# Gating the weight transfers of a DeltaNet and Fourier-mixing kernel on TensorE's instruction packets, in a hand-written list scheduler

## The chip, the cores and the metric

The kernel runs on one core of one Trainium2 chip. The metric is the device time of one launch in microseconds; lower is better. TensorE (PE) does the matrix products, VectorE (DVE), ScalarE (ACT) and GpSimd (POOL) the elementwise work, and SyncE (SP) issues nearly all transfers from and to HBM. Each engine runs its own instruction list in the order in which it was written.

## The reference

Two blocks follow each other. The first is a delta-rule attention over 4 batches, 8 heads, 768 positions and a head size of 48; the second mixes its output (4 x 768 x 384) with a two-dimensional Fourier transform, normalizes it and runs a two-layer MLP.

```python
k_n = k / (np.linalg.norm(k, axis=-1, keepdims=True) + 1e-06)
for t in range(S):
    y[:, :, t] = np.einsum('bhd,bhde->bhe', q[:, :, t], state)
    v_old = np.einsum('bhde,bhd->bhe', state, kt)
    state = state + bt[:, :, :, None] * np.einsum('bhd,bhe->bhde', kt, vt - v_old)
...
mixed = np.real(np.fft.fft(np.fft.fft(x, axis=1), axis=2))
u = x + mixed
un = (u - mu) / np.sqrt(var + 1e-06)
ch = np.maximum(un @ w_ch1, 0.0) @ w_ch2
return (u + ch).astype(np.float32)
```

The weights `w_ch1` (384 x 1536) and `w_ch2` (1536 x 384) come as 64-bit floats, which the chip turns into 32-bit ones by integer arithmetic; everything else is float32.

## The kernel before

The sequence of each batch is cut into six units of 128 positions, each of two chunks of 64; there are 24 units. A unit loads its k, q and v (192 KB each, `load`), transposes them on TensorE (`turn`, line 467), builds small triangular systems for the heads (`keys`, `gram`), inverts them on DVE (`invert16`, `invert`) and then runs the recurrence chunk by chunk (`chain0`, `values0`, `outputs0` for the first six units, `step` and `outputs` for the others). When a batch's units are done, `mixing` runs its Fourier transform (`folds`, `seq`, `feat`), normalizes (`normed`) and runs the MLP in three groups of 256 rows (`mlp`; the last batch's `mlpw`). An MLP group takes six blocks of the first layer (12 matmuls of 128x256 in the trace each) and six of the second; the blocks of the first layer are evicted by a Relu at line 1459.

Nothing of this is written in the order in which it runs. Each function hands its pieces to a planner, `Plan.op`, with the engines that could run it, an estimated duration, the memory that it reads and writes, a due time, the size of a transfer (`kb`) or the number of TensorE instructions (`ni`). `Plan.schedule` then simulates all engines at build time, picking for each free engine the most urgent piece that is ready, and `issue` writes the instructions out in that order. All matmuls go through the helper lines 464 and 467, all copies through 473 and 475. The order is fixed when the kernel is built; on the chip the semaphores decide when each instruction goes.

Parts of the planner that the change touches:

- `Plan.fetch` models TensorE's instruction packets: 256 instructions each. A packet is asked for when TensorE has gone AHEAD = 128 instructions past a boundary and is there FETCH = 3.4 us later; TensorE cannot pass the next boundary before.
- `Plan.speed` and `Plan.work` model TensorE's clock by stretches of 3.413 us; `Plan.light` tells when TensorE has had little work in the last 2.6 us.
- `idle` (lines 1899 to 1914) writes filler matmuls on constants into a spare PSUM bank: groups of six at the very start (line 1906, 12 matmul rows in the trace), a pair on 64 rows or a single one on 128 rows later (line 1913). They compute nothing that is used. The planner adds one where TensorE has nothing ready and its load is light.
- TARGET, FORCE, GAP, GAP2, HALF, PLOOK, PEND, HOLD and the due-time constants M0 to MD are numbers that steer these choices.

The weights are brought in by `weights`, 18 pieces of 512 columns, nine for each matrix, in the order w1, w2, w1, w2, w1, w2 by thirds. A piece is transferred as 64-bit words into a staging slot (512 KB, on SP, line 512; in two transfers where it crosses a row block), and converted by six operations: ACT (1675), DVE (1678), ACT (1681), DVE (1686), POOL (1691) and DVE (1694). The staging slots are parts of tiles that are not in use yet: seven for the first NW = 14 pieces (`ws`, two in `x`, four in the tiles R1 and R0), and then three (`ws` and two in `x`). A transfer is written in SP's order at the place where the planner found its slot free; in the program it waits for the last reader of the slot.

```python
stages = [(ws, 0), (xs[1], 0), (xs[1], 1024), (R1, 2304), (R1, 3328), (R0, 0), (R0, 1024)]

def where(nw):
    return stages[nw[0] % 7] if nw[0] < NW else stages[(nw[0] - NW) % 3]
```

Of the kernel before, what the change touches and what calls it, by code (L numbers as in the profile page):

```python
# [14 lines left out]
ACT = mybir.ActivationFunctionType  # L15
# [9 lines left out]
class Op:  # L25
    __slots__ = ("i", "engs", "fn", "deps", "succ", "pr", "mode", "banks", "new", "lat",
                 "ndep", "ready", "start", "end", "eng", "due", "kb", "col", "ni", "hot", "port")
# [3 lines left out]
RATE = 190.0  # L31
WIN, WARM, COLD, BUSY, CLOCK = 3.413, 610.0, 619.0, 200.0, True
LOOK, HOLD, EARLY = 1e9, 0.2, 25.7
FOLD, BY, SEQ, HOT, HOTPE, HOTPK, HOTG, NORM = 1, 1, 2, 1.0, 1, 1, 0, 1
HOTC, PORT, E2 = 2, 1, 5.0
GAP, HALF = 0.15, 90.0
GAP2 = 0.324
PLOOK, PHOLD, PEND = 22.2, 0.367, 110.0
NHALF = 1
FORCE = 546.3  # L40
BLOCK, AHEAD, FETCH = 256, 128, 3.4
TARGET, SPANW = 725.1, 2.6


class Plan:
# [10 lines left out]
    def op(self, engs, fn, rd=(), wr=(), pr=0.0, mode=None, new=None, use=(), lat=0.0,  # L56
           due=1e9, kb=0, col=0, ni=0, port=False):
# [5 lines left out]
        o.due, o.kb, o.col, o.ni, o.hot, o.port = due, kb, col, ni, self.hot, port  # L63
        o.banks = list(use) + new
# [55 lines left out]
    def fetch(self, o):  # L120

        n0, n1 = self.count, self.count + o.ni
        for k in range((n0 - AHEAD) // BLOCK + 1, (n1 - AHEAD) // BLOCK + 1):

            t = o.start + (o.end - o.start) * (k * BLOCK + AHEAD - n0) / o.ni
            self.come.append(max(t, self.come[-1]) + (FETCH if t > 12 else 7.0))
        for k in range(n0 // BLOCK + 1, n1 // BLOCK + 1):
            if k < len(self.come):
                o.end = max(o.end, self.come[k] + (o.end - o.start) * (n1 - k * BLOCK) / o.ni)
        self.count = n1  # L130
# [19 lines left out]
    def schedule(self, pick, limits, switch, idle=None, span=()):  # L150
# [26 lines left out]
        self.count, self.come = 64, [0.0, 0.0]  # L177
        done, n, now = 0, len(ops), 0.0
        order, strict, last = [], True, None
        while done < n:  # L180
            progressed = False
            for e in self.ENG:
# [4 lines left out]
                if e != "PE":  # L187
                    cand = [o for o in cand if not any(b.busy > now + 1e-9 and (not BY or b.by != e)
                                                       for b in o.banks)]
                if e == "PE":  # L190
# [42 lines left out]
                elif cand:  # L233
                    if PORT and e == "DVE" and free["POOL"] > now + 1e-9:
                        cand = [o for o in cand if not o.port]
# [19 lines left out]
                dur = o.engs[e]  # L255
                if e == "PE":
                    dur *= self.speed(now)
                    if mode is not None:
                        dur += switch.get((mode, o.mode), 0.0)
                    mode = o.mode  # L260
                    for b, s in zip(o.new, fr[len(o.new), o.mode] if o.new else ()):
                        b.slot, slots[s] = s, None
                        self.half = {k: x for k, x in self.half.items() if x != s}
                        held[b.cls] = held.get(b.cls, 0) + 1
                o.start, o.end, o.eng = now, now + dur, e
                if o.kb:

                    o.end = max(now, landed[-8]) + dur
                    moved = max(moved, o.end) + o.kb / RATE
                    landed.append(moved + o.lat)  # L270
                    o.lat = landed[-1] - o.end
# [94 lines left out]
def kernel(  # L366
# [90 lines left out]
    def eng(e):  # L457
        return {"DVE": nc.vector, "POOL": nc.gpsimd, "ACT": nc.scalar, "SP": nc.sync}[e]

    def I(x):  # L460
        kp(x)
# [54 lines left out]
    M0, MP, MX, MN, MA, MT, MD = 100.7, 138.9, 27.6, 31, 25, 7.59, 5.46  # L516
# [1128 lines left out]
    def weights(src, dst, rows, cols, where, pr, pieces=None):  # L1645
# [10 lines left out]
        for c0 in pieces:  # L1656
# [6 lines left out]
            rr = st[:, 0:2 * n:2]  # L1663
            done = 0
# [44 lines left out]
    NW, IV, IV1, WP = 14, 9.46, 10, -25.4  # L1709
# [152 lines left out]
    mixing(0)  # L1862
    for ro in ros[2:]:
        if ro is ros[-1]:
            tables(0)
        prepare(ro)
        consume(ro)

    LIM = {"state": 1, "sum": 4, "attn": 6, "mix": 4, "mlp": 4, "norm": 2, "win": 4}
    WAIT, GATHER, URGENT, FIRST = 5.62, 1.92, 12.1, 10.3  # L1870
    E0, E1, D1 = 1.0, 10.0, 115.0
# [79 lines left out]
```

## Time and profile before

| what | us |
|---|---|
| runs, median of 3 | 677.76 (676.92 to 678.70) |
| profiled execution | 683.04 |
| its span, first to last instruction | 681.2 |
| mean granted TensorE clock over the span | 0.980 |
| first MLP matmul of the first batch (line 464, w and R) | 132.03 |
| last conversion step of a weight (line 1694) | 142.8 |

The profile describes one profiled execution. Its times count from the span's first instruction. "Granted clock" is the share of full speed that TensorE's clock was given in a stretch. A view by stretches cuts the span at given times and tells how long each engine was busy in each. In the view of waits, "<- issue" means that the engine stood still and that the profile shows no semaphore that it waited for. PE's rows count matmuls, PEld its weight loads; in this trace a float32 matmul of the program stands as two matmul and two load rows. SPq is the queue in which SP issues transfers. Queues 8 and 14 of the DMA engines carry instructions, queue 1 the kernel's data. The trace also has the start of each single DMA packet by queue.

### The profile page before, as it was taken

The numbers are of one execution on the slowest core, as the hardware profiler recorded it, in microseconds if no ns is written. First come the engines' busy times: TensorE is split into PE (matmuls) and PEld (weight loads), VectorE is DVE, ScalarE is ACT, GpSimd is POOL, SyncE is SP. The second block draws the span as 40 slices with busy tenths as digits, with TensorE's granted clock in tenths as the row PEclk, the third lists the DMA queues.
The fourth block names the chain that finished last, engine by engine and source line by source line (L and its number), as shares of the span: only waits on it lengthen the run. The fifth ranks groups of instructions, "written<-read, shape, count | busy, mean of one in ns | idle before, by whom it ended". The sixth has DMA issues, their size and how long they took to land.

```text
span 681.2 us, 22852 instructions
## 1 busy us (share of the span) xinstructions
PE 665.9 (98%) x10028; PEld 535.5 (79%) x10028; DVE 471.8 (69%) x1365; ACT 265.3 (39%) x739; POOL 34.0 (5%) x34
## 2 busy tenths in 40 slices
PE   7999979999999999999999999999999999999998
PEld 7778879867777777877777869776877778899997
DVE  3999467999996268999962546999995433823133
ACT  5679575622344324522433514322523412311110
POOL 3013321100000000000000000000000000000000
PEclk9999696999999999999999999999999999999999
DMA  9925465000032212000312210000000000000000
GB/s 215 276 76 132 87 162 137 2 1 1 25 62 51 58 26 50 24 1 2 72 38 48 61 37 13 24 2 1 27 1 4 26 1 1 24 1 24 0 25 23
DMA packets 82581, 31.33 MB, mean 46 GB/s; under 512 B 75569, under 2 KB 79634, under 8 KB 82354
## 3 DMA queue, kind: packets, MB, share of 16 engines
q1 hardware_dynamic: 82290, 29.65, 17.6%
q8 instruction: 78, 1.28, 0.8%
q10 hardware_dynamic: 192, 0.23, 0.1%
q14 instruction: 21, 0.17, 0.1%
HBM read 25.16 MB, written 4.72 MB: 44 GB/s over the span
## 4 chain that ended last, share of the span: by engine, by line
PE 92%; DVE 4%; issue 2%; ACT 2%; DVEq 0%; ACTq 0%
PE pp L464 87%; PE pp L467 3%; PE pp L1913 1%; DVE tmp L839 1%; DVE w L845 1%; PE pp L1906 1%; ACT us L473 1%; DVE rr L862 0%; DVE rr L735 0%; DVE rr L779 0%; DVE w L805 0%; DVE us L698 0%; ACT L1723 0%; ACT w L473 0%; DVE w L812 0%
## 5 line engine op out<-in xcount | busy, mean ns | idle before, releaser
L464 PE MATMUL pp<-R,w 128*128 128x256 f32 x864 | 203.5, 387 | 0.6 <-ACT R L473 0.6
L464 PEld LDWEIGHTS pp<-R,w 128*128 128x128 f32 x864 | 161.2, 191 | 24.1 <-ACT R L473 0.7
L464 PE MATMUL pp<-w,R 128*128 128x384 f32 x432 | 151.8, 495 | 0.0
L464 PEld LDWEIGHTS pp<-w,R 128*128 128x128 f32 x432 | 79.0, 190 | 46.0 <-issue 0.2
L1459 ACT ACTIVATE R<-pp 128x512 f32<-128x512 f32 x54 | 32.2, 597 | 132.4 <-PE pp L464 128.5
L473 ACT ACTIVATE us<-pp 128x256 f32<-128x256 f32 (+3 forms) x165 | 58.2, 393 | 42.9 <-PE pp L464 24.7
L464 PE MATMUL pp<-us 64*64 64x48 f32 (+3 forms) x2496 | 63.1, 238 | 2.8 <-issue 2.8
L464 PEld LDWEIGHTS pp<-us 64*64 64x64 f32 (+1 forms) x2496 | 53.6, 137 | 9.5 <-issue 7.0
L922 DVE TENSOR_TENSOR rr<-rr,tmp 128x210 f32<-128x210 f32 (+11 forms) x180 | 58.3, 327 | 3.4
L917 DVE TENSOR_TENSOR tmp<-rr 128x210 f32<-128x210 f32 (+12 forms) x180 | 58.1, 326 | 3.0
L464 PEld LDWEIGHTS pp<-u,us 64*64 64x64 f32 x1472 | 41.9, 138 | 19.0 <-issue 16.9
L464 PE MATMUL pp<-u,us 64*64 64x48 f32 x1472 | 48.2, 225 | 3.8 <-issue 3.3
L1174 DVE TENSOR_TENSOR u<-u,pp 64x192 f32<-64x192 f32 x66 | 22.5, 350 | 34.6 <-PE pp L464 31.6
L1238 DVE TENSOR_TENSOR x<-x,pp 64x192 f32<-64x192 f32 x66 | 23.2, 352 | 29.2 <-PE pp L464 28.1
L473 ACT ACTIVATE x<-pp 64x192 f32<-64x192 f32 (+1 forms) x81 | 25.0, 324 | 44.4 <-PE pp L464 39.7
L1572 DVE TENSOR_TENSOR gd<-us 128x128 f32<-128x128 f32 x36 | 8.9, 289 | 48.0 <-ACT us L1557 48.0
L473 ACT ACTIVATE R<-pp 128x192 f32<-128x192 f32 (+6 forms) x81 | 23.2, 338 | 39.1 <-PE pp L467 19.5
L1557 ACT ACTIVATE us<-pp 128x512 f32<-128x512 f32 x18 | 10.7, 597 | 61.3 <-PE pp L464 61.3
L464 PE MATMUL pp<-tab,R 128*96 128x193 f32 (+2 forms) x192 | 34.0, 336 | 0.1
L1913 PE MATMUL pp<-pack 64*64 64x256 f32 (+1 forms) x214 | 32.8, 406 | 0.5 <-ACT x L473 0.3
L464 PEld LDWEIGHTS pp<-tab,R 128*96 128x96 f32 (+2 forms) x192 | 31.9, 168 | 1.0 <-DVE x L1493 0.2
L464 PEld LDWEIGHTS pp<-st,us 48*64 48x64 f32 x1232 | 23.4, 138 | 11.6 <-issue 10.0
(151 smaller groups left out, 879.6 us busy)
## 6 DMA issues: line engine op xcount, KB each, us to landing
us<-in_k_dram SPq DMA_DIRECT2D x24, 192.0 KB, 3.7
us<-in_q_dram SPq DMA_DIRECT2D x24, 192.0 KB, 3.5
us<-in_v_dram SPq DMA_DIRECT2D x24, 192.0 KB, 3.7
out_dram<-x SPq DMA_DIRECT2D x11, 384.0 KB, 2.5
R<-in_moe_w_ch_dram SPq DMA_DIRECT2D x3, 512.0 KB, 5.0
ws<-in_moe_w_ch_dram SPq DMA_DIRECT2D x3, 512.0 KB
x<-in_moe_w_ch_dram SPq DMA_DIRECT2D x3, 512.0 KB, 5.7
tab<-k_tab SPq DMA_DIRECT2D x1, 1155.0 KB, 7.7
```

What stands on the lines that cost most here:

```text
L464: I(nc.tensor.matmul(o, lhsT=lhsT, rhs=rhs, start=start, stop=stop, skip_group_check=True))
L467: I(nc.tensor.matmul(o, lhsT=src, rhs=ident[p0:p0 + n, p0:p0 + n], is_transpose=True, start=start, stop=True, skip_group_check=True))
L473: I(nc.scalar.activation(o, i, ACT.Copy, **({} if scale is None else {"scale": scale})))
L839: I(eng(e).tensor_tensor(T_, sub(j + 1, 16, j, j + 1).broadcast_to([128, 2, n, j]), sub(j, j + 1, 0, j).broadcast_to([128, 2, n, j]), op=A ...
L917: I(eng(e).tensor_tensor(T_, R[:, :, j + 1:32, j:j + 1].broadcast_to([128, ns, n, j]), R[:, :, j:j + 1, 0:j].broadcast_to([128, ns, n, j]) ...
L922: I(eng(e).tensor_tensor(R[:, :, j + 1:32, 0:j], R[:, :, j + 1:32, 0:j], T_, op=ALU.add))
L1174: I(nc.vector.tensor_tensor(U[:, s], U[:, s], psum(b1[s])[a, s0:s1].rearrange("p (j d) -> p j d", d=D), op=ALU.subtract))
L1238: I(nc.vector.tensor_tensor(w, w, v, op=ALU.add))
L1459: I(nc.scalar.activation(o, s, ACT.Relu))
L1557: I(nc.scalar.activation(o, s, ACT.Relu))
L1572: vec(128, lambda e, j=j, i0=i0, i1=i1, op=op: I(nc.vector.tensor_tensor(s(j), i0, i1, op=op)), [aH] + rd, [aS(j)], pr - EV)
L1913: I(nc.tensor.matmul(pst[two[0]][x, 0:256], lhsT=w[x, 0:n], rhs=w[x, 0:256], start=True, stop=True, skip_group_check=True))
```

## The change

Three things change: a gate ahead of every weight transfer, the model of instruction packets, and the constants.

The gate is one more operation per piece: a write of one column (128 x 1) into the staging slot, by ACT (`activation` Copy of a constant) or by DVE (`memset`). The transfer that follows writes the same column, so it waits for the gate. The planner lets a gate go only when `Plan.open` says so: after GMIN = 33 us of its time, when the packet asked for last has begun to come (`seek`), when no gate has gone in the present packet and when TensorE still has more than GROOM = 110 instructions to go until it asks for the next one; after GMAX = 119 us of its time, always.

The packet model asks for a packet LEAD = 60 instructions ahead of a boundary, one at a time, takes SEEK = 1.0 us until its transfer begins and LAND = 2.4 us until it is there, and holds it up by as much as HOLDUP = 2.5 us where a data transfer is under way (`bursts`).

Up to LATE = 17.3 us of its time the planner lets PE, DVE and ACT take only operations that were handed in before the third round of units. NW goes from 14 to 8, so that ten of the 18 pieces use the three last slots. The other constants get new values.

```diff
-LOOK, HOLD, EARLY = 1e9, 0.2, 25.7
+LOOK, HOLD, EARLY = 1e9, 0.185, 25.7
-GAP, HALF = 0.15, 90.0
-GAP2 = 0.324
-PLOOK, PHOLD, PEND = 22.2, 0.367, 110.0
+GAP, HALF = 0.155, 92
+LATE = 17.3
+GAP2 = 1.47
+PLOOK, PHOLD, PEND = 30.9, 0.367, 117.2
-FORCE = 546.3
-BLOCK, AHEAD, FETCH = 256, 128, 3.4
-TARGET, SPANW = 725.1, 2.6
+FORCE = 477.6
+BLOCK, LEAD, SEEK, LAND, HOLDUP = 256, 60, 1.0, 2.4, 2.5
+GATE, GROOM, GMIN, GMAX = 1, 110.3, 33.0, 119.0
+TARGET, SPANW = 729.4, 2.6
...
     def fetch(self, o):
 
         n0, n1 = self.count, self.count + o.ni
-        for k in range((n0 - AHEAD) // BLOCK + 1, (n1 - AHEAD) // BLOCK + 1):
-
-            t = o.start + (o.end - o.start) * (k * BLOCK + AHEAD - n0) / o.ni
-            self.come.append(max(t, self.come[-1]) + (FETCH if t > 12 else 7.0))
+        while BLOCK * (len(self.come) - 1) - LEAD < n1:
+            x = max(BLOCK * (len(self.come) - 1) - LEAD, n0)
+            t = o.start + (o.end - o.start) * (x - n0) / o.ni
+            t = max(t, self.come[-1]) + SEEK
+            for a, z in self.bursts:
+                if a <= t < z:
+                    t = min(z, t + HOLDUP)
+                    break
+            self.seek = t
+            self.come.append(t + LAND)
         for k in range(n0 // BLOCK + 1, n1 // BLOCK + 1):
-            if k < len(self.come):
-                o.end = max(o.end, self.come[k] + (o.end - o.start) * (n1 - k * BLOCK) / o.ni)
+            o.end = max(o.end, self.come[k] + (o.end - o.start) * (n1 - k * BLOCK) / o.ni)
         self.count = n1
+
+    def open(self, now):
+
+        k = len(self.come)
+        return (now > GMAX or now > GMIN and
+                self.seek <= now + 0.7 and self.gated != k and
+                BLOCK * (k - 1) - LEAD - self.count > GROOM)
...
+                if now < LATE and e in ("PE", "DVE", "ACT"):
+                    cand = [o for o in cand if o.i < self.next]
...
+                    if e in ("DVE", "ACT") and not self.open(now):
+                        cand = [o for o in cand if not o.gate]
...
+                if o.i >= 0 and o.gate:
+                    self.gated = len(self.come)
...
+                    self.bursts.append((moved - o.kb / RATE + 1.0, moved + 0.7))
+                    self.bursts = self.bursts[-6:]
...
-    M0, MP, MX, MN, MA, MT, MD = 100.7, 138.9, 27.6, 31, 25, 7.59, 5.46
+    M0, MP, MX, MN, MA, MT, MD = 94, 144.2, 29, 33.7, 6.03, 6.75, 5
...
             rr = st[:, 0:2 * n:2]
+            def gate(e, w=st[:, 0:1]):
+                if e == "ACT":
+                    I(nc.scalar.activation(w, half, ACT.Copy))
+                else:
+                    I(eng(e).memset(w, 0.0))
+            if GATE:
+                P.op({"ACT": 0.16, "DVE": 0.07}, gate, [A(half, 0, 1)], [a0], pr, lat=0.1, gate=True)
...
-    NW, IV, IV1, WP = 14, 9.46, 10, -25.4
+    NW, IV, IV1, WP = 8, 9.46, 10.4, -25.4
...
     mixing(0)
+    P.next = len(P.ops)
     for ro in ros[2:]:
...
-    WAIT, GATHER, URGENT, FIRST = 5.62, 1.92, 12.1, 10.3
-    E0, E1, D1 = 1.0, 10.0, 115.0
+    WAIT, GATHER, URGENT, FIRST = 4.24, 1.97, 13.3, 11.7
+    E0, E1, D1 = 0.3, 10.0, 122.4
```

## The prediction

> **What bounds the kernel now.** I read the page's busy rows and slices first.
>
> ```profile
> span 681.2 us, 22852 instructions
> PE   665.9 (98%) x10028; PEld 535.5 (79%) x10028; DVE 471.8 (69%) x1365; ACT 265.3 (39%) x739; POOL 34.0 (5%) x34
> ...
> PEclk9999696999999999999999999999999999999999
> DMA  9925465000032212000312210000000000000000
> ...
> q8 instruction: 78, 1.28, 0.8%
> ```
>
> TensorE is busy 98% of the span, so the end is set by how much it has to do and how much of its time is wasted. Waste is idle time, half clock and filler matmuls. The slices below 9 in the clock row lie in the first 17% of the span, where DMA is busy too. Queue 8 carried 78 packets of 16 KB; TensorE's rows (10028 matmuls and as many weight loads) are 20056, or 257 a packet: these are its instructions. Next the waits of TensorE, and its time by stretches that I cut along the steps of the granted clock:
>
> ```profile
> PE pp L464 <- issue: 8.6, 8, 2.2
> ...
> 62.12:65.53 3.41, 3.02 (x124) 2.72 (x123) 3.41 (x7) 3.16 (x10) 1.29 (x1) 1.00 0.66 165
> 65.53:68.95 3.42, 2.24 (x93) 2.08 (x85) 1.01 (x3) 2.34 (x6) 3.05 (x3) 1.00 0.78 202
> 68.95:79.19 10.24, 9.88 (x200) 8.89 (x200) 4.60 (x12) 4.76 (x13) 0.00 (x0) 0.50 0.22 43
> 89.43:92.84 3.41, 2.37 (x80) 2.12 (x71) 2.21 (x5) 2.25 (x7) 1.29 (x1) 1.00 0.86 213
> 99.67:103.08 3.41, 1.75 (x67) 1.62 (x59) 3.41 (x8) 0.99 (x3) 1.54 (x1) 1.00 0.66 153
> 103.08:113.32 10.24, 10.24 (x159) 9.35 (x156) 9.09 (x26) 6.04 (x21) 1.96 (x1) 0.50 0.57 145
> 283.99:287.40 3.41, 2.33 (x36) 1.78 (x28) 3.38 (x14) 2.42 (x10) 0.00 (x0) 1.00 0.01 2
> 287.40:290.81 3.41, 3.40 (x8) 2.77 (x9) 3.41 (x13) 0.33 (x1) 0.00 (x0) 0.50 0.00 0
> ```
>
> Columns: stretch and length, PE, PEld, DVE, ACT, POOL busy, granted clock, DMA share, GB/s. TensorE waited eight times, 8.6 us in all, for nothing that the profile shows ("issue"). Where a stretch of 3.41 us had only 2.24 or 1.75 us of TensorE work, the next 10.24 us ran at clock 0.50; 2.33 cost 3.41 us of it, and 2.37 cost none. The timelines of TensorE and of SP's queue show the largest two holes and what was in flight:
>
> ```profile
> 69.31 0.63 PE L464 MATMUL pp<-us,pb 64*32 64x32 f32 x14 [1.53 <-issue]
> 102.05 1.22 PE L464 MATMUL pp<-u,us 64*64 64x48 f32 x33 [1.66 <-issue]
> ...
> 61.78 2.99 SPq L512 DMA_DIRECT2D R<-in_moe_w_ch_dram  x2
> 66.02 0.38 SPq L512 DMA_DIRECT2D us<-in_v_dram  x1
> ...
> 96.61 0.34 SPq L512 DMA_DIRECT2D ws<-in_moe_w_ch_dram  x1
> 99.51 0.37 SPq L512 DMA_DIRECT2D us<-in_v_dram  x1
> ```
>
> The trace has each packet of queue 8 with its start. The packets that ended holes began at 67.01 and 99.64 us, and TensorE went on 2.30 and 2.41 us later; the other holes fit at 2.3 to 2.7. With DMA quiet a packet begins about 1.1 us after TensorE has come to some 60 instructions before the end of the packet ahead of it; these two came 3.9 and 3.2 us after that point, with the other queues busy 3.0 and 1.8 us of it. So the holes are late instruction packets, late behind transfers.
>
> **What the change does, and the sum.** It starts from the profiled execution: 681.2 us of span, 683.04 us in all, so 1.8 us lies around the span. The runs' median is 677.76, 5.3 us less; I take the change in the span over to the median unaltered.
>
> (1) Holes behind weights. Of the eight, those at 67.77, 87.87, 91.80 and 100.39 us (1.53, 0.62, 1.40, 1.66) had a packet that weight transfers of 256 to 512 KB ran into. Every weight transfer now waits for a column written just after a packet was asked for. Gain 5.2 us if all four go; 0 if the writes miss. The first hole (2.24 us at 11.19) I keep: the q and v loads around it stay ungated. The other three (0.19, 0.55, 0.40) sat behind k, q and v loads of 192 KB, also ungated; kept.
>
> (2) Half clock. The two stretches of 10.24 us at 0.50 each lose 5.12 us, 10.2 together, and TensorE has work without a break in both (9.88 and 10.24 busy). They follow (1)'s two longest holes; without these, 3.42 less what short idle remains is far over 2.37. Gain 10.2; 0 if other holes of that size arise. The half clock at 287.40 (1.7 us lost) follows waits for ACT (0.50 and 0.59): the new order puts three fillers of the 128-row form among the transforms around it, where there was none; between 0 and 1.7, taken as 0.
>
> (3) Fillers. By the instruction order there are four more pairs of the 64-row form, two more of the 128-row form and one more start group (12 matmul rows). From the timeline: 60 records in 7.78 us is 0.52 a pair; four records in 1.13 us is 0.57; 48 records in 4.32 us is 1.08 a start group. Full price 2.1 + 1.1 + 1.1 = 4.3 us; 0 where TensorE would have idled anyway. The start group stands ahead of the first k load's work, which TensorE awaits anyhow, and the 128-row ones sit at (2)'s ACT waits; I take 2.1 for the rest.
>
> (4) The writes: 16 on ACT, two on DVE. Nearest rows: a 128x1 ACT activation takes 170 to 289 ns (L473, L1381), a 128x1 DVE memset 59. At most 16 x 0.29 = 4.6 us on ACT. From 30 to 130 us ACT is busy 71.6 of 100 us, so most are hidden by its own idle time; it is full (9.0 and 9.6 of 10) from 40 to 60, where four or so fall and PSUM evictions stand behind them: 0.5 us, bounds 0 and 4.6.
>
> (5) Waits of the writes. Eleven on ACT wait for the Pool add (L1691, about 1.5 us) that last read the staging slot; behind them in ACT's queue stand evictions (L473, L1459) that release TensorE's banks. Late by a third of such an add once or twice: 0.5 us; bounds 0 and 11 x 1.5 = 16.5 us.
>
> (6) Weights later. SP now issues all 18 q, k, v loads and both tables ahead of any weights, where ten weight transfers went in the first 30 us; and a k, q or v load behind a gated transfer on SP waits with it. The last four pieces stand, in ACT's order, behind the first evictions of the MLP (L1459). A piece needs 2.9 to 5.0 us to land and 0.68 + 0.69 (ACT) + 0.52 + 0.43 + 0.82 (DVE) + 1.5 (POOL) = 4.6 us to convert: at most 9.6. The first MLP matmuls run at 132.03, and the blocks that read the last third of w1, which the late pieces fill, at 156.71: 24.7 us later, less 9.6 makes a cover of about 15 us. Price 0; without the cover, rival C.
>
> After 140 us TensorE is 100% busy at clock 1.00 but for the 287 us spot, and its work is the same. Sum: -5.2 - 10.2 + 2.1 + 0.5 + 0.5 = -12.3: span 668.9, and 677.76 - 12.3 = **665.5 us** by the median.
>
> The Trainium skill says otherwise twice. "Runtime: NRT & Kernel Launch", section Instruction fetch mechanics, holds that the sequencer fetches the next page while it runs the current one and that crossing a 16 KB boundary is "mostly hidden". The trace does not agree in this stage: holes up to 1.66 us end 2.3 us after a packet begins. By that rule term (1) is zero and, with it, (2). "TensorE: Matmul & The Clock Gate", section HAM oscillation, asks only that no idle gap exceed about 3.4 us; here 1.53 us sufficed. By it (1) stays and (2) is zero.
>
> **Rivals.**
> A. One hole of that size comes back, behind k, q and v loads, which stay ungated and now crowd together, or in a packet a gated transfer overlaps: 1.5 + 5.1 = 6.6 us returned, 672.1. For it: three holes sat behind such loads; against: none was over 0.55.
> B. The drops of the clock are not from packets, or fall elsewhere: only (1) pays, -5.2 + 3.1 = -2.1: 675.7. Against: both drops start in the step after the hole.
> C. Slower. The last weights are too late. Gates are crossed in order by ACT; if ACT lags so that the last pieces start more than (6)'s cover behind, TensorE stands still in the first MLP blocks, as its order is fixed. Three staging slots serve the last ten pieces at up to 9.6 us a round; a lag of one such round beyond the cover (9.6 us) plus two stretches of half clock (10.2) makes -12.3 + 19.8 = +7.5: 685.3. It decides from 2.1 us of standstill on (with the two drops). Against: in the trace TensorE had no wait for weights, and the last L1694 ended at 143.5.
> D. The writes do not hold the transfers: holes stay as before, weights merely move: +3.1: 680.9. Against: in the program SP's first transfer of every piece waits on ACT or DVE.
>
> **How the numbers follow.** Forecast 0.60, A 0.18, B 0.07, C 0.10, D 0.05. A measurement of this kernel tells 0.3%, or 2 us, from no change: 675.7 to 679.8 is the same. Faster: forecast, A, half of B: 0.82; same: the other half of B and a little of D: 0.05; slower: C and most of D: 0.13. The forecast's own range is 658 to 671: below by the remaining 1.1 of holes, 1.7 of clock at 287, 2.1 of fillers, 1.0 of (4) and (5) and 1.5 of the first hole; above by 2.2 us more fillers, 1.7 us of writes and 1.5 us of holes. To hold eight in ten it reaches over A up to 676, and 1 us lower, to 657, for the spread of the runs (676.92 to 678.70 now).
>
> **What would show it.** Right: "issue" waits of TensorE under 4 us, no stretch of 10.24 us at clock 0.50 after 20 us, records of the filler of L1913 about 16 + 4 = 20 more than 214, first MLP matmul some 12 us before 132.03. (5) wrong: TensorE waits for ACT in the first 130 us beyond the 1.7 us of now. (6) wrong: TensorE waits for the final DVE step of a weight. The prediction falls if clock 0.50 shows again between 60 and 120 us.

## The result, and the profile after

The changed kernel takes 681.22 us (median of 20 runs, 679.03 to 689.64); the kernel before, run beside it on the same chip, takes 677.42 (20 runs, 674.78 to 684.33). The ratio is 1.0059, with a 95% interval of 1.0037 to 1.0080: it is slower by about 4 us. The forecast was 665.5 us, with a range of 657 to 676. All ratios here, and the means of rest and clock further down, leave out the few runs that took over 1.5% longer than the fastest of the same kernel; the medians hold all runs.

The profiled execution after took 683.72 us, 681.9 of them span, nearly the same as the profiled execution before (683.04 and 681.2). Here are the head of its page, the clock, the instruction queue and the chain that ended last:

```profile
span 681.9 us, 22911 instructions
...
PE 665.0 (98%) x10060; PEld 532.1 (78%) x10060; DVE 465.9 (68%) x1359; ACT 269.2 (39%) x763; POOL 32.7 (5%) x34
...
PEclk9999899999999999989999999999999999999999
...
q8 instruction: 79, 1.29, 0.8%
...
PE 79%; DVE 15%; ACT 3%; issue 3%; ACTq 0%
```

The row of the chain before:

```profile
PE 92%; DVE 4%; issue 2%; ACT 2%; DVEq 0%; ACTq 0%
```

TensorE is busy 98% of the span, as before. The clock row has lost the low digits (6 and 6) of the front and shows an 8 in the fifth and in the 18th slice, near 70 and near 290 us. DVE's share of the chain that ended last has grown from 4% to 15%. TensorE's waits:

```profile
PE pp L488 <- issue: 6.1, 4, 2.3
PE pp L488 <- DVE t L974: 2.4, 1, 2.4
```

Lines have moved: what was 464 is 488, 950 is 974, 1694 is 1725, 1913 is 1945. The holes that are late instruction packets went from 8.6 us to 6.1, and a wait of 2.4 us for DVE is new. What went is the first hole, of 2.24 us near 12 us, which the prediction kept. The holes between 48 and 105 us take as long as before: 6.35 us in seven then, 6.13 us in four now. The stretches around three of the four drops of the clock (columns: stretch, length, then the busy time of PE, PEld, DVE, ACT and POOL with the number of instructions, clock, DMA share, GB/s):

```profile
68.28:71.69 3.41, 1.12 (x29) 1.00 (x27) 1.36 (x3) 1.76 (x5) 1.28 (x1) 1.00 0.68 151
71.69:75.10 3.41, 3.41 (x87) 3.41 (x85) 1.09 (x3) 1.42 (x5) 0.00 (x0) 0.50 0.32 62
95.58:98.99 3.41, 1.63 (x76) 1.50 (x71) 2.17 (x7) 1.93 (x7) 1.08 (x1) 1.00 0.60 115
98.99:102.41 3.42, 3.42 (x41) 3.16 (x38) 2.06 (x5) 1.20 (x4) 0.21 (x1) 0.50 0.84 237
180.91:184.32 3.41, 1.45 (x65) 1.39 (x66) 3.41 (x10) 0.90 (x3) 0.31 (x1) 1.00 0.03 7
184.32:187.73 3.41, 3.41 (x6) 1.69 (x5) 3.31 (x11) 0.81 (x3) 0.00 (x0) 0.50 0.00 0
```

Two drops follow holes in the front (ending at 70.79 and 98.52 us), as before, but each lasted 3.41 us and not 10.24. The third follows the new wait for DVE. The fourth, at 290 us, is the one that was at 287. A drop of 3.41 us that the kernel before had at 14.34 us, behind its first hole, is gone.

To see where the time went, I split TensorE's span from the trace into filler matmuls (lines 1906 and 1913, now 1938 and 1945), time without any matmul, and the rest, which is the kernel's own work; of that work I take off what the half clock added.

| us of the profiled span | before | after |
|---|---|---|
| own work at full clock | 621.4 | 621.8 |
| added to it by the half clock | 11.3 | 6.4 |
| fillers | 33.2 | 36.8 |
| no matmul | 15.3 | 16.9 |
| sum | 681.2 | 681.9 |

So, in these two executions, 4.9 us less of the own work were lost to the clock, and 3.6 us of fillers, 1.6 us of idle time and 0.4 us of work came in. The fillers' 33.2 us hold 2.1 us of half clock too (0.4 of the 36.8 after), so at full clock the fillers grew by 5.3 us. But this execution of the kernel before was an unusual one. Every timed run has its span and mean granted clock. I call span x (1 - clock) the loss to the clock, and span x clock the rest (work, fillers and idle time). The profiled execution before had a clock of 0.980: 13.6 us lost. In the 104 runs of the kernel before that were timed beside the experiments the clock was never under 0.982; its mean was 0.989 to 0.992 in the four sets of runs, a loss of 5.6 to 7.4 us. The changed kernel lost 5.2 us on average in the runs of its result. A gain by the clock is therefore in this pair of profiles, and not in the medians, where the rest alone has grown.

### The profile page after: what moved, and what is told of

Read it like the earlier page. It is cut to its first block, busy times and chain, and to the rows that moved or that the text cites. A ratio compares the mean times of both kernels' runs of the same rounds, so it can differ in the third digit from the quotient of the medians.

```text
span 681.9 us, 22911 instructions
## 1 busy us (share of the span) xinstructions
PE 665.0 (98%) x10060; PEld 532.1 (78%) x10060; DVE 465.9 (68%) x1359; ACT 269.2 (39%) x763; POOL 32.7 (5%) x34
## 3 DMA queue, kind: packets, MB, share of 16 engines
q8 instruction: 79, 1.29, 0.8%
## 4 chain that ended last, share of the span: by engine, by line
PE 79%; DVE 15%; ACT 3%; issue 3%; ACTq 0%
PE pp L488 74%; PE pp L491 2%; DVE tmp L941 2%; PE pp L1945 2%; DVE rr L946 2%; ACT us L497 1%; PE pp L1938 1%; DVE w L869 1%; DVE rr L759 1%; DVE us L722 1%; DVE tmp L863 1%; DVE w L1725 1%; DVE us L704 1%; DVE pm L1417 0%; ACT w L1706 0%
## 5 line engine op out<-in xcount | busy, mean ns | idle before, releaser
L488 PE MATMUL pp<-w,R 128*128 128x384 f32 x432 | 154.3, 501 | 0.2 <-ACT R L1483 0.2
L1483 ACT ACTIVATE R<-pp 128x512 f32<-128x512 f32 x54 | 32.1, 596 | 116.5 <-PE pp L488 109.6
L497 ACT ACTIVATE us<-pp 32x256 f32<-32x256 f32 (+3 forms) x168 | 60.1, 399 | 37.8 <-PE pp L488 22.0
L488 PE MATMUL pp<-us 64*64 64x48 f32 (+3 forms) x2496 | 61.3, 235 | 0.1
L941 DVE TENSOR_TENSOR tmp<-rr 128x168 f32<-128x168 f32 (+11 forms) x180 | 59.5, 335 | 2.7
L946 DVE TENSOR_TENSOR rr<-rr,tmp 128x168 f32<-128x168 f32 (+11 forms) x180 | 58.9, 332 | 2.5
L497 ACT ACTIVATE R<-pp 128x192 f32<-128x192 f32 (+7 forms) x79 | 22.7, 338 | 41.2 <-PE pp L491 24.4
L1945 PE MATMUL pp<-pack 64*64 64x256 f32 (+1 forms) x230 | 34.6, 391 | 0.1
```

Source lines behind the costliest of these rows:

```text
L488: I(nc.tensor.matmul(o, lhsT=lhsT, rhs=rhs, start=start, stop=stop, skip_group_check=True))
L497: I(nc.scalar.activation(o, i, ACT.Copy, **({} if scale is None else {"scale": scale})))
L941: I(eng(e).tensor_tensor(T_, R[:, :, j + 1:32, j:j + 1].broadcast_to([128, ns, n, j]), R[:, :, j:j + 1, 0:j].broadcast_to([128, ns, n, j]) ...
L946: I(eng(e).tensor_tensor(R[:, :, j + 1:32, 0:j], R[:, :, j + 1:32, 0:j], T_, op=ALU.add))
L1483: I(nc.scalar.activation(o, s, ACT.Relu))
L1945: I(nc.tensor.matmul(pst[two[0]][x, 0:256], lhsT=w[x, 0:n], rhs=w[x, 0:256], start=True, stop=True, skip_group_check=True))
```

## The experiments

All were run beside the kernel before on the same chip; "rest" and "clock" are the differences of the mean rest and of the mean loss to the clock from it.

| run | median us | before beside it | ratio (95%) | rest | clock |
|---|---|---|---|---|---|
| changed kernel again (e5) | 681.53 | 676.87 | 1.0075 [1.0050, 1.0099] | +3.9 | +1.2 |
| gates not issued (e1) | 681.19 | 676.14 | 1.0082 [1.0056, 1.0109] | +3.9 | +0.9 |
| late DVE steps out (e2) | 677.61 | 676.14 | 1.0040 [1.0011, 1.0069] | +3.5 | -1.5 |
| and late POOL steps out (e3) | 677.30 | 676.14 | 1.0037 [1.0013, 1.0060] | +2.2 | -0.8 |
| late DVE steps out of before (e4) | 678.95 | 676.14 | 1.0040 [1.0018, 1.0061] | +1.9 | +0.8 |
| late transfers out (e6) | 682.75 | 676.87 | 1.0076 [1.0043, 1.0109] | +2.6 | +2.3 |
| late transfers out of before (e7) | 671.91 | 676.87 | 0.9926 [0.9901, 0.9951] | -0.7 | -4.0 |
| added fillers out (e8) | 680.35 | 676.87 | 1.0046 [1.0015, 1.0077] | +3.0 | 0.0 |
| model alone, old constants (e9) | 683.77 | 676.44 | 1.0106 [1.0062, 1.0150] | +6.3 | +1.0 |
| model and gates, old constants (e10) | 685.18 | 676.44 | 1.0129 [1.0086, 1.0172] | +9.1 | -0.2 |
| model and new constants, no gates (e11) | 687.83 | 676.44 | 1.0174 [1.0130, 1.0218] | +8.3 | +3.6 |
| gates until 90 instead of 119 (e12) | 684.51 | 676.44 | 1.0103 [1.0057, 1.0148] | +8.4 | -1.2 |
| before, FETCH 3.3 (e13) | 677.64 | 679.36 | 0.9982 [0.9956, 1.0008] | +2.0 | -3.6 |
| before, HOLD 0.185 (e14) | 686.54 | 679.36 | 1.0129 [1.0081, 1.0177] | +2.3 | +5.2 |
| before, new constants (e15) | 680.39 | 679.36 | 1.0030 [0.9995, 1.0065] | +0.8 | +0.6 |
| changed, LEAD 58 (e16) | 683.45 | 679.36 | 1.0065 [1.0030, 1.0100] | +4.1 | -0.1 |

The standard errors of the differences are 0.4 to 0.8 us for the rest and 0.6 to 1.6 us for the clock.

### Do the gate writes cost anything, and do they help? (e1, e5)

The planner's order is left as it is; only the writes are not issued, so that each transfer starts as soon as its slot is free.

```diff
         for o in self.order:
-            o.fn(o.eng)
+            if not getattr(o, 'gate', False):
+                o.fn(o.eng)
```

> The changed kernel in its own order, with the 18 one-column writes not issued; all else stands where it stood. Theory T (late weights): the cost of the change is DVE work moved into 120 to 183 us, which this order keeps, and the writes themselves only guard the packets. Then the DVE wait of TensorE near 181 us stays (2.4 us in the profile of after), the holes behind late packets grow from 6.1 us to about 8 to 10, and the time is 0 to 8 us above the changed kernel's 681.2. Rival W (the writes): ACT stands in the writes and in their waits for POOL; then it is 3 to 6 us faster than the changed kernel, 675 to 678. Rival C (constants): the time is that of the changed kernel within 2 us.

> The changed kernel once more, for its clock in each run and a second profile. Span x granted clock was 668.6 us on average over 29 runs of the kernel before and 674.6 over 19 of the changed one, while the loss to the clock (span x (1 - clock)) was 5.8 and 5.2. If that holds, the change does nothing for the clock in the ordinary run, and adds some 6 us of idle time and fillers: 680 to 682 here, loss 4 to 7, the rest 673 to 676.

Without the writes the rest stands 3.9 us over the kernel before, with them 3.9: neither a cost nor a help that could be measured (the error of this comparison is 0.7 us). The "issue" waits did not grow to 8 to 10 us either; they are 4.9 us in e1's profile, against 6.1 with the writes. TensorE's wait of 2.4 us for DVE stays.

### Why holes remain behind a gate (e6, e7)

The trace of the changed kernel has each DMA packet with its start. SP's queue between 48 and 66 us, where the first gated transfers run (columns: start, length, what SP issued, and how many):

```profile
50.25 0.33 SPq L536 DMA_DIRECT2D ws<-in_moe_w_ch_dram  x1
50.67 4.59 SPq L536 DMA_DIRECT2D us<-in_v_dram  x2
56.67 0.82 SPq L536 DMA_DIRECT2D R<-in_moe_w_ch_dram  x2
57.59 0.38 SPq L536 DMA_DIRECT2D us<-in_k_dram  x1
60.27 0.33 SPq L536 DMA_DIRECT2D x<-in_moe_w_ch_dram  x1
64.27 0.38 SPq L536 DMA_DIRECT2D us<-in_q_dram  x1
65.18 0.33 SPq L536 DMA_DIRECT2D x<-in_moe_w_ch_dram  x1
```

Every transfer waits for its gate: one instruction packet begins at 49.50 us, the gate's write comes at 50.03, SP issues the weight transfer at 50.25, and its data moves from 51.23 on. But the ungated v, k and q loads stand right behind it in SP's queue, and the transfers run into one another. From the starts and ends of the data packets:

| data moving | length | size | instruction packets in it: late by | hole of TensorE that they ended |
|---|---|---|---|---|
| 51.23 to 54.32 us | 3.09 | 704 KB | 3.18 | 1.11, to 56.74 us |
| 57.65 to 63.44 | 5.79 | 1216 KB | 4.13 and 3.32 | 0.95, to 65.42 |
| 65.31 to 71.41 | 6.10 | 1088 KB | 4.51 and 4.29 | 2.29, to 70.79 |
| 92.41 to 96.17 | 3.77 | 704 KB | 2.48 | 1.78, to 98.52 |
| 96.80 to 102.74 | 5.94 | 1088 KB | 4.59 | none |

"Late by" is counted to the packet's start from the point at which it is asked for, as far as the trace tells; with DMA quiet it is about 1.1 us. Counted from the holes, that point lies some 60 instructions before the boundary ahead of the one that the packet opens, that is some 316 instructions before the packet is needed; the prediction's words "before the end of the packet ahead of it" place it one packet too late, though its times were counted as here. TensorE goes on 2.3 to 2.6 us after the packet's start. In this stage TensorE comes to that point every 3.8 to 5.1 us (at 50.95, 54.74, 59.79, 63.85 and 67.63). A burst that is about as long or longer meets the next packet however exactly its first transfer was placed.

Nor are all gates placed as the planner meant. It lets a gate go when the packet asked for last has begun or is to begin within 0.7 us. On the chip these four gates went while a packet had been asked for and not begun (TensorE came to its points at 54.74, 59.79, 63.85 and 96.11; the packets began at 58.87, 63.11, 68.37 and 100.70):

```profile
56.45 0.20 ACT L1690 ACTIVATE R<-eps 128x1 f32<-128x1 f32 x1
60.18 0.06 DVE L1692 MEMSET x<- 128x1 f32 x1
64.95 0.20 ACT L1690 ACTIVATE x<-eps 128x1 f32<-128x1 f32 x1
97.47 0.22 ACT L1690 ACTIVATE x<-eps 128x1 f32<-128x1 f32 x1
```

The gated transfers behind them moved ahead of those packets. In the second profile of the changed kernel (e5) the same four gates came too early, by 1.0 to 3.9 us. The planner's packet model holds a packet up by at most 2.5 us; here packets began as much as 4.59 us after they were asked for, 3.5 us more than with DMA quiet. No run tells how much of the loss is these gates and how much the k, q and v loads.

How much is there to win? In e6 and e7 the transfers of pieces 8 to 18 are not issued, in the changed kernel and in the one before.

```diff
-    def dma(o, i, wr, pr, rd=(), kb=200, q="SP"):
+    def dma(o, i, wr, pr, rd=(), kb=200, q="SP", go=True):
         def fn(e):
+            if not go:
+                return
...
-                    [A(w0[0], w0[1] + 2 * done, w0[1] + 2 * done + 2 * m)], pr, kb=m)
+                    [A(w0[0], w0[1] + 2 * done, w0[1] + 2 * done + 2 * m)], pr, kb=m,
+                    go=nw[0] <= 7)
```

> The changed kernel in its own order, the transfers of weight pieces 8 to 18 left out; all their writes and conversions stay (on the data that the slot still holds, so these weights are wrong). It bounds what perfect gating could bring. Theory P (packets behind weights cost what the profile of before suggested): the issue waits fall from 6.1 us to 2 or less and the loss to the clock from 5 to 2 or less: 6 to 9 us faster, 672 to 675. Theory N (k, q and v loads and the rate of the packets themselves keep most holes; the clock is lost elsewhere): 0 to 3 us faster, 678 to 681. The DVE wait at 181 us stays in both.

> The kernel before in its own order, the transfers of pieces 8 to 18 left out in the same way. Theory P, with the 15.4 us that the prediction booked: 662 to 668. Theory N: 673 to 676, no more than 3 us below the kernel before on the same chip, since its ordinary run loses 5.8 us to the clock and not the 13.6 of the profile of before.

The waits and the clock of e7:

```profile
span 669.5 us, 22800 instructions
...
PEclk9999999999999999899999999999999999999999
```

```profile
PE pp L464 <- issue: 3.5, 8, 1.2
```

In the kernel before, all collisions with these weight transfers together are worth about 5.0 us, 4.0 of them by the clock; that lies between the two theories. It is about what perfect gates could have brought in that order (and more than they alone, since no conversion waits for these transfers either); my steps (1) and (2) had 15.4. In the changed kernel the same edit brought nothing: pieces 1 to 7 and the k, q and v loads now fall into this stage, and data still moved almost without a break from 57.38 to 63.59 us (1216 KB) and from 64.39 to 70.14 (1088 KB), and holes of 1.50 and 1.74 us ended at 65.05 and 69.88.

### The late conversions (e2, e3, e4)

TensorE's timeline of the changed kernel where the new wait is:

```profile
182.87 1.20 PE L488 MATMUL pp<-t,us 64*32 64x32 f32 x64 [2.42 <-DVE t L974]
184.00 4.54 PE L488 MATMUL pp<-w,R 128*128 128x384 f32 x8
```

The group of eight matmuls took 4.54 us instead of 2.85, because it ran at half clock. What TensorE waited for is no weight but the inverse of the next chunk. DVE makes it, and DVE has no time to spare. From 120 to 183 us, in the kernel before and then in the changed one (columns as in the stretches above):

```profile
120.00:183.00 63.00, 62.86 (x509) 47.32 (x508) 60.31 (x176) 24.41 (x73) 3.58 (x4) 1.00 0.02 8
```

```profile
120.00:183.00 63.00, 60.34 (x408) 44.61 (x410) 62.18 (x171) 25.58 (x72) 8.77 (x7) 1.00 0.15 49
```

DVE is busy 62.18 of 63 us. (That alone does not make the wait: in e15, further down, DVE is busy 62.33 of the same 63 us, and TensorE has no such wait.) Three more weights are converted in this stretch (six final steps against three), and six POOL adds run in it against three (the last POOL row of each count is a memset). Where one runs, DVE's inverse stands still as well:

```profile
151.64 0.33 DVE L946 TENSOR_TENSOR rr<-rr,tmp 128x168 f32<-128x168 f32 x1
152.00 1.35 DVE L941 TENSOR_TENSOR tmp<-rr 128x184 f32<-128x184 f32 x1
153.39 0.35 DVE L946 TENSOR_TENSOR rr<-rr,tmp 128x184 f32<-128x184 f32 x1
```

```profile
151.86 1.29 POOL L1722 TENSOR_TENSOR w<-w,ws 128x512 int32<-128x512 int32 x1 [2.91 <-DVE w L1717]
```

An operation of 0.35 us took 1.35 and ended just behind the add. The Trainium skill, "SBUF — State Buffer", section SBUF: two separate sides, describes a port pair that a DVE operation with two SBUF inputs and a GpSimd operation that reads SBUF hold in turn, each for a whole instruction. This trace agrees: 1.35 us beside an add of 1.29.

In e2 the three DVE steps of the last six pieces are left out, in e3 their POOL step too, and in e4 the DVE steps in the kernel before, as a control.

```diff
             nw[0] += 1
+            late = nw[0] > 12
...
-            P.op({"DVE": 0.38}, f1, [], [ac], pr, lat=LD, port=True)
+            P.op({"DVE": 0.38}, (lambda e: None) if late else f1, [], [ac], pr, lat=LD, port=True)
```

> The changed kernel in its own order, but the three DVE steps of the last six weight pieces are left out (18 DVE instructions; the weights of these pieces are wrong), ACT's and POOL's steps stay. Theory T: DVE is the bound from 120 to 183 us; with some 18 instructions and about 9.5 us of DVE work less, the wait of 2.4 us at 181 us and the half-clock stretch behind it (1.7 us) go, and the filler work of the second mixing shrinks: 4 to 7 us faster than the changed kernel, 674 to 677. Rival W: no more than 1 us faster. Rival C: as W, since the order of everything else is the same.

> As the run before, with POOL's step of the last six pieces left out too. In the profile of after the DVE instructions that meet such a POOL step take 1.0 to 1.35 us in place of 0.3. If that is part of the cost, this is another 0 to 2 us faster than with the DVE steps alone left out; if DVE has room again by then, the same within 1 us.

> Control: the kernel before, in its own order, with the three DVE steps of the last six pieces left out. There these steps end at 89 to 143 us, three of the six pieces after 120 us, and TensorE waits for no DVE at 180 us. Theory T: less gain than in the changed kernel, 0 to 2 us against 677.4. If DVE work is worth as much here as there (4 to 7 us), its place in time is not the cause.

TensorE's timeline of e2 at the same place:

```profile
179.76 1.20 PE L488 MATMUL pp<-t,us 64*32 64x32 f32 x64
180.90 2.85 PE L488 MATMUL pp<-w,R 128*128 128x384 f32 x8
```

The wait is gone, and the eight matmuls run at full clock. The median is 3.6 us under that of e1 beside it, which has the same order with all its conversions; the same cut in the kernel before (e4) gains nothing, and even comes out slower by its interval. So in this order the late conversions bring the wait and the half clock behind it, and leaving them out makes the kernel faster. How the gain divides is less sure: of the difference to e1, 2.4 us stand as clock (-1.5 against +0.9) and 0.4 as rest (1.7 in e3), with errors of 0.7 for the rest and over 1 for the clock. In e4 less work made the rest 1.9 us larger, so shifts of that size happen with an order kept. What e3 adds to e2 can't be told from nothing in the medians.

### The fillers (e8)

One start group and the three fillers among the second batch's transforms are not written.

```diff
         def fn(e):
+            if now < 0.5 or 240 < now < 290:
+                return
             if now < E2:
```

> The changed kernel in its own order without one of its five start groups of fillers and without the three that it has in the second mixing, near 250 to 290 us. If fillers lie on TensorE's path at full price: 1.1 + 3 x 0.5 = 2.6 us faster, 678 to 679. If TensorE would stand idle there anyway, no change, or slower by 1.7 us where a stretch falls to half clock.

By the rows 2.6 us of matmuls were taken away, and the rest fell by about 1.0 us (672.5 against 673.5 in e5, each to within 0.4). So by the means they were paid for by less than half, and the remainder would have been idle time; with an error of 0.5 to 0.6 us on that 1.0, nothing at all or most of the price is not ruled out.

### One part of the change at a time (e9 to e12)

The code of the change, with the constants of before and without gates (e9) or with them (e10); with the new constants and no gates (e11); and with all parts, the gates open to all from 90 instead of 119 us on (e12).

```diff
-GATE, GROOM, GMIN, GMAX = 1, 110.3, 33.0, 119.0
+GATE, GROOM, GMIN, GMAX = 0, 110.3, 33.0, 119.0
```

> The new packet model in the planner, without gates and with the old constants: ten weight transfers are again issued ahead of the inversion, in the first 30 us, and no conversion ends late. By the theory that has stood so far (late weights cost DVE time and fillers, gates win nothing): no DVE wait of over 1 us near 180 us, span x clock (idle time and fillers) 668 to 671, time 675 to 679. If it is the new model's order that is worse: rest 673 or more and 680 or more.

> The same with the gates: all 18 pieces are transferred after the inversion, as in the changed kernel, with the old constants. The theory: 3 to 6 us slower than the same without gates, by idle time and fillers and not by the clock; 679 to 684. If the gates do protect packets: faster than without them, with a loss to the clock under 3 us in place of 5 to 6. If the changed kernel's cost lay in its constants: the same as without gates within 1.5 us.

> The changed kernel's constants and model, planned without gates: weights early again. The theory: 675 to 679, rest 669 to 672, no DVE wait near 180 us. If the constants are the cost: 680 to 684, as the changed kernel.

> The changed kernel with GMAX = 90 in place of 119, so that the gates stop holding earlier; three pieces rather than five have their last step in the stretch in which DVE is full. The order is nearly that of the changed kernel. The theory: DVE wait near 180 us of 0.5 to 1.5 us in place of 2.4, 1 to 2 us faster than the changed kernel: 678.5 to 680.5.

The theory missed in all four: against the kernel before, every mixture came out slower than the changed kernel itself, e11 clearly, the other three with intervals that overlap e5's. In e9 it was the rival that came true, that the new model's order is worse: 683.77 us, and a rest of 675.6. In e11 the last weight is converted at 121 us, early, and it is still the slowest. So gates and late weights are not the bulk of it. Nor are late weights needed for the wait. In e9, whose last final step starts at 116.5 us, TensorE waits as long for the same line, later:

```profile
316.39 1.20 PE L488 MATMUL pp<-t,us 64*32 64x32 f32 x64 [2.53 <-DVE t L974]
```

The fillers' rows point to something that the mixtures share. In e9, with line numbers as in the changed kernel:

```profile
L1945 PE MATMUL pp<-pack x236: 374/376/631, 16.0 to 677.9; 64*64 64x256 f32 x104, 128*128 128x256 f32 x14
```

Columns are the shortest, median and longest duration in ns, first and last start, and the forms. Before there were 214 such records. By the split used above, fillers take 39.0 us in e9, 37.7 in e10, 38.4 in e11 and 37.9 in e12, against 33.2 before and 36.8 after; together with the idle time it is 53.7 to 57.3 us against 48.5. But each of these kernels also has an order made anew, with constants that were chosen for another model. That is the question of the next four.

### Is it the new model, or any new order? (e13 to e16)

Three orders from the old planner, without gates: one number of its packet model moved a little (e13), one threshold moved to its new value (e14), and all the new constants (e15). And one order from the new planner with all its parts (e16).

```diff
-BLOCK, AHEAD, FETCH = 256, 128, 3.4
+BLOCK, AHEAD, FETCH = 256, 128, 3.3
```

> The kernel before, with FETCH = 3.3 instead of 3.4: the old packet model, no gates, the old constants; only the planner's order changes, from about the place of the inverse of the first units on (three more TensorE rows in the program). Theory X (the loss is in the new model and its gates: they bring more fillers and idle time; an order from the old model has neither): 675 to 678.5 us, the part of the span that does not go to the clock within 1.5 of the 669.4 us of the kernel before, fillers of 32 to 35 us. Theory Y (the order of before was an uncommonly good one; any order made anew by the same planner is 3 to 8 us slower, whichever model makes it): 680 to 685 us, that part at 672.5 or more.

> The kernel before, with HOLD = 0.185 (the value of the change) instead of 0.2, and nothing else: a new order, four more TensorE rows. Theory X: 676 to 680 us (one or two us more fillers, as more pairs stand in the front), the part outside the clock 669 to 672. Theory Y: 680 to 685 us, that part 672.5 or more.

> The kernel before with the constants of the change (NW = 8, the due times, HOLD, GAP, GAP2, PLOOK, FORCE, TARGET, WAIT and the rest), but with the old packet model and no gates. Theory X: 675 to 679 us, and no more idle time than before; if below 675 it would be the version that beats both. Theory Y: 680 to 685 us. Theory Z (the constants carry the loss: ten pieces through three slots put conversions late under the MLP): 679 to 683 with TensorE waiting for DVE near 180 us.

> The changed kernel with LEAD = 58 instead of 60: the same model, gates and constants, another order (one filler fewer in the program). Theory X: 679 to 683 us, like the changed kernel. Theory Y: slower than the changed kernel too, 682 to 687 us, as the changed kernel's order would be an uncommonly good one for its model.

By the bare times e15 and e16 fall into the ranges of theory Y, but the kernel before stood at 679.36 us beside these runs, about 2 to 3 us above the other sets, so the differences are what counts. The two parts of the span behave differently. The rest goes with the model: three orders from the old model stand 0.8 to 2.3 us over the kernel before, and all orders with the new model that leave nothing out 3.9 to 9.1. The new constants alone (e15) cost nothing in it that could be told. That is theory X, in a weaker form: a new order alone costs up to about two microseconds too.

The profiles show where a part of this lies. TensorE's busy time from 120 to 400 us is the first number after the length; the rows are before, e15, after and e9:

```profile
120.00:400.00 280.00, 278.70 (x4288) 213.19 (x4287) 218.02 (x625) 107.82 (x308) 4.51 (x7) 0.99 0.15 33
120.00:400.00 280.00, 278.05 (x4338) 212.49 (x4338) 215.93 (x626) 104.75 (x301) 5.08 (x6) 1.00 0.16 35
120.00:400.00 280.00, 275.96 (x4245) 210.64 (x4246) 219.98 (x625) 110.89 (x314) 9.71 (x10) 0.99 0.18 43
120.00:400.00 280.00, 275.92 (x4242) 210.18 (x4243) 210.18 (x610) 105.34 (x302) 1.25 (x4) 0.99 0.15 33
```

So it has no matmul for 1.3 us before and for 1.8 to 2.1 in e13 to e15, but for 4.0 to 6.4 in every order with the new model that leaves nothing out (after, e5, e9 to e12, e16). Most of that is waits for DVE, with late weights and without. The fillers tell less: by the split above they take 33.6, 37.7 and 34.5 us in e13, e14 and e15, and 37.6 in e16.

The loss to the clock goes with neither model: e13 and e14 have the same model and differ from the kernel before in one number each, and they lose 3.8 and 12.6 us to it. The clock of e14, whole rows of its page and of two stretches:

```profile
PEclk9898889999999999999999999999999999999999
```

```profile
58.41:61.82 3.41, 1.68 (x65) 1.57 (x65) 2.89 (x2) 1.71 (x4) 0.86 (x2) 1.00 1.00 294
61.82:72.06 10.24, 10.24 (x232) 10.11 (x231) 7.31 (x14) 6.72 (x19) 3.08 (x3) 0.50 0.30 57
```

This is what I had seen in the profile before: a stretch with 1.68 us of TensorE's work, then 10.24 us at half clock. A threshold of the planner that has to do with neither packets nor weights made the order in which it happens. By the medians that order cost 7.2 us, 5.2 of the mean loss being clock. By its time alone e14 would have spoken for theory Y.

No run that computes everything was faster than the kernel before by more than its interval.

## Why the prediction was wrong

**The basis** failed first. I saw that the profiled execution stood 5.3 us over the median and carried the change "in the span over to the median unaltered". Those 5.3 us were the half clock itself: the profiled execution lost 13.6 us to it, an ordinary run of the same kernel 5.6 to 7.4. Most of what step (2) was to gain had no place in the median; leaving out the late transfers altogether gained 4.0 us by the clock (e7).

**(2), half clock, -10.2.** Wrong, and the largest error. In the runs of its result and in e5 the changed kernel lost 5.2 and 6.8 us to the clock; the kernel before lost 5.6 beside e5. The 10.24 us are not a fixed price either. After the hole at 70.79 us with only 1.12 us of work in the stretch, the clock was back after 3.41 us; in e14 1.68 us of work cost 10.24. The clause that the prediction set for its own fall, clock 0.50 between 60 and 120 us, came true at 71.7 and 99.0.

**(1), holes behind weights, -5.2.** Wrong: of the four holes that it counted on, about nothing was gained. From 48 to 105 us the holes take 6.13 us in place of 6.35 (and 6.34 in e15, which has the new constants and no gates). "Issue" waits fell from 8.6 to 6.1 us, not under 4, and what fell is the first hole, of 2.24 us, which I had kept. I saw q and v loads around it, but five weight transfers went out there as well, from 7.6 to 11 us. Gates alone shrink it, from 2.36 us in e9 to 0.40 in e10; the new constants without gates remove it too (e15). I priced every gated transfer by itself. But the transfers merge with k, q and v loads into bursts of 3.1 to 6.1 us, where a packet is asked for every 3.8 to 5.1; and four gates went while a packet had been asked for and not begun. The first is the mechanism of rival A, which I gave one hole. Rival D had the outcome, that holes stay and weights merely move, and with 680.9 us the nearest number; its cause is not what happened, as every transfer waited for its write. Even without any late transfer e7 has 3.5 us of such waits left.

**(3), fillers, +2.1.** The count was right: 238 records of the later fillers against 218 and one more start group. Their time in the profile grew by 3.6 us as it stands and by 5.3 at full clock, more than the 2.1 and, at full clock, than the full price of 4.3. By e8 those that it left out cost about 1.0 us of 2.6, to within 0.6.

**(4) and (5), the writes and their waits, +1.0.** Small, as predicted; a cost of 1.0 us would hardly show. A write on ACT took 0.19 to 0.30 us, and e1 without them has the same rest, to within 0.7. TensorE's waits for ACT stayed at about 2 us.

**(6), weights later, price 0.** This step failed by its cover. The 15 us were TensorE's: no weight came too late for a matmul. The engine that had no time was DVE. The prediction shows its load for the whole span alone, 69%, and not for the stage, where the profile before already had it busy 60.31 of 63 us. Rival C named a standstill in the first MLP blocks through late weights, and it gave 685.3. It had the direction right and the kind wrong: TensorE waited 2.4 us for an inverse, not for a weight. Nor did the first MLP matmul come 12 us earlier; it ran at 126.67 instead of 132.03.

**The sum.** Of the 15.7 us between the forecast and the median after, about 10 are the clock (-10.2 predicted, +1.2 found in e5, -0.1 in e16) and about 6 the rest: -2.1 predicted (-5.2 + 2.1 + 1.0), +3.9 found in e5, +4.1 in e16. The prediction had no term for what a new order does to the rest, and that is the step that is missing. In these two profiles the larger rest is fillers and idle time: 53.7 us after against 48.5 before. Of the new idle time, the wait of 2.42 us is shown to come from the late conversions (e2); the start group with the three fillers is a likely part, about 1.0 us. Why every order of the new model lets TensorE wait more for DVE after 120 us, and why most ask for more fillers too, was not followed further: the cause of the larger rest stays open.

The two rules of the Trainium skill would have given a better number than the trace as I read it, by luck. By "Runtime: NRT & Kernel Launch", Instruction fetch mechanics, (1) and (2) are zero, and the medians came out nearer to that than to my sum. Yet the rule does not agree with these traces: packets left TensorE standing for up to 2.29 us after and 3.0 us in e13. By "TensorE: Matmul & The Clock Gate", HAM oscillation, (2) is zero; it came out near zero, but not because short gaps are harmless: the wait of 2.42 us at 180.45 us brought the half clock at 184.31.

## What to carry to other kernels

Before a gain is taken from one profiled execution, compare its clock with that of the timed runs: a stretch of half clock that only the profile has is not there to be won. A transfer that is moved has to be priced with what stands behind it in its queue and with the engine that has to work on it, in the stage where it arrives. With a planned order any edit makes a new order, and here such orders differ by up to 9 us among themselves; a part of a change can be judged only against that scatter, best by a run that keeps the order and leaves the part out. Even then, differences of up to 2 us came from less work (e4).

## What the hardware showed that was not expected

- The same kernel loses between 0 and 12 us to the clock from run to run (granted clock 1.00 to 0.982 over 104 runs of the kernel before, 0.980 in its profiled execution), and orders that differ from it in one number 3.8 to 12.6 us on average.
- How long the half clock lasts does not follow the size of the hole: 1.12 us of work in a stretch of 3.41 us was followed by 3.41 us of it, 1.68 us by 10.24 (e14).
- An instruction packet begins about 1.1 us after TensorE has come to some 316 instructions before it is needed with DMA quiet, and up to 4.59 us after that point behind a data burst.
- A DVE operation of 0.35 us took 1.35 us beside a POOL addition, and the POOL addition its ordinary 1.29.
